# A small sum of the softmax, written as a two-operand addition or as a sum along the free axis, in an attention and feed-forward kernel

## The chip, the core and the metric

The kernel runs on one core of one Trainium2 chip. The metric is the device time of one launch in microseconds; the median of three runs before the change is 1084.55 us (1083.58 to 1084.83). The engines are named as the profile names them: PE is the matrix engine and PEld its weight loads, DVE the vector engine, ACT the scalar engine, POOL the GpSimd engine, SP the queue that issues nearly all DMAs.

## The reference

Causal attention with a decay, over 8 batches, 8 heads, 576 positions and a head size of 64, feeds a gated feed-forward layer (4608 tokens, 512 to 2048 to 512).

```python
scores = scale * np.matmul(q, k.transpose(0, 1, 3, 2))
cum = np.cumsum(np.log(np.clip(f, 0.0001, 1.0)), axis=-1)
decay = cum[:, :, :, None] - cum[:, :, None, :]
scores = np.where(causal, -1000000000.0, scores + decay)
scores = scores - np.max(scores, axis=-1, keepdims=True)
attn = np.exp(scores)
attn = attn / (np.sum(attn, axis=-1, keepdims=True) + 1e-09)
...
h = x @ w_in
sp = np.maximum(h, 0.0) + np.log1p(np.exp(-np.abs(h)))
return ((h * erf(sp)) @ w_out).astype(np.float32)
```

The change is in one place of it: the addition of 1e-09 to the sums of the exponentials, ahead of the division.

## The kernel before, in words

The launch has two stages. The first, up to about 331 us of the trace, is the attention. The second is the feed-forward layer, whose matmuls fill the rest.

The attention walks over 64 steps t. Two heads make a pair p, and each pair has two steps: an even one with the query blocks 4 and 1 (half 0) and an odd one with the blocks 3, 2 and 0 (half 1); j names the head of the pair. The work of one step is spread over several rounds of the loop `for t in range(NH + 2)`, so that in one round the engines work on different steps:

- `scores(t)` on PE (L528, L535) writes the scores of both heads into two PSUM buffers `s`.
- `reduce(t, j)` on DVE (L559) adds the decay, takes the running minimum and writes the scores to the SBUF tile `pr`. Its row extremum goes to part 0 of the small tile `st`. Each L559 is followed by a short read of the accumulator under the same line.
- `exps(t - 1, j)` on ACT (L571) makes the exponentials in place and writes their row sums to part 1 of `st`.
- `normalize(t - 2)` on DVE adds 1e-9 to part 1 (L576) and writes the reciprocals to part 2 (L578); then POOL multiplies `pr` by them (L582).
- `transposes(t - 3, a)` on PE (L594) and `evacuate` on ACT (L599, L603) or DVE (L601) bring the probabilities to the tile `pt`.
- `values(t - 4)` on PE (L621) multiplies by the values into the one PSUM buffer `o`.
- `store(t - 5)` on DVE copies `o` to the SBUF tile `xo` (L630 after an even step's result, L633 and L634 after an odd one's), and SP sends `xo` to DRAM.

Beside this the weights of the feed-forward layer are put together from 64-bit words: DVE runs `words` (L377 to L379) and `joined` (L386, L395), POOL subtracts and adds (L406, L414, L424), ACT rounds (L401, L418). This is called conversion work below. From step 23 on POOL and ACT also prepare the first inputs of the feed-forward layer (L132, L138, L143).

All engines run their instructions in the order in which the loop writes them; no scheduler moves them. On DVE one round is: `normalize`, `store`, `reduce(t, 0)`, `reduce(t, 1)`, in odd rounds an L601, then conversion work if some is due. In this order an instruction that is late on DVE makes all behind it late.

`st` is one tile of 32 columns for each step, with two buffers for each half. Its first 6n columns (n = 2 or 3 blocks) are read as three parts of 2n. The constant is a tile `edge` of 24 columns, set once at the start (L336).

Of the kernel before, what the change touches and what calls it, by code (L numbers as in the profile page):

```python
# [11 lines left out]
F32 = mybir.dt.float32  # L12
# [4 lines left out]
ALU = mybir.AluOpType  # L17
# [5 lines left out]
P = 128  # L23
# [11 lines left out]
BLOCKS = [[4, 1], [3, 2, 0]]  # L35
# [32 lines left out]
SOFTPLUS = "softplus"  # L68
MASK = -2.0 ** 33

EDGE = 24
BIG = 3.0e38

TINY = 2.0 ** -15
# [240 lines left out]
def attention_moe(ctx, tc, q2, k2, vp, f, w_in, w_out, out):  # L315
    nc = tc.nc
# [15 lines left out]
    upper = const.tile([P, P], BF16, name="upper")  # L332
    nc.vector.tensor_copy(out=upper, in_=low)
    edge = ctx.enter_context(tc.tile_pool(name="edge", bufs=1, side="right"))
    tiny = edge.tile([P, EDGE], F32, name="edge")
    nc.vector.memset(tiny, 1e-9)  # L336
    cum_d = dram.tile([B * H, S], F32, name="cum_d")
    xt_d = [dram.tile([DM, NW], F32, name=f"xt_d{v}") for v in range(NV)]

# [121 lines left out]
    with ExitStack() as ph:  # L461
        early = ExitStack()
        wk = ph.enter_context(tc.tile_pool(name="wk", bufs=2))
# [14 lines left out]
        pairs, stats, probs, vals, raw_scores, pts, banks, held = {}, {}, {}, {}, {}, {}, {}, {}  # L478
# [40 lines left out]
        def scores(t):  # L519


            p, half = divmod(t, 2)
            q, k = pairs[p][:2]
            s = [ps_s.tile([P, 1024], F32, name=f"s{t}_{j}", tag="s") for j in range(2)]
            for at, i, k0, k1 in PARTS[half]:
                for j in range(2):
                    h = slice(64 * j, 64 * j + 64)
                    nc.tensor.matmul(out=s[j][:, at:at + k1 - k0], lhsT=q[h, PAD + START[i]:PAD + END[i]],  # L528
                                     rhs=k[h, k0:k1], start=i > 0, stop=k1 < END[i] or i == 4 and p > 0)
            for j in range(2):  # L530
                for i in BLOCKS[half]:
                    if i == 3 or i == 4 and p:
                        continue
                    first = max(0, START[i])
                    nc.tensor.matmul(out=s[j][:, SCOL[i] + first:SCOL[i] + END[i]], lhsT=eye,  # L535
                                     rhs=upper[:, first - START[i]:], start=False, stop=True)
            raw_scores[t] = s
            probs[t] = wk.tile([P, TCOLS[half]], F32, name=f"pr{t}", tag=f"pr{half}")
            n = len(BLOCKS[half])
            line = wk.tile([P, 32], F32, name=f"st{t}", tag=f"st{half}")  # L540
            stats[t] = line[:, :6 * n].rearrange("p (a j m) -> p a j m", a=3, j=2)

        def mask(p, i):

# [4 lines left out]
        def row(t, i, j):  # L549

            return probs[t][:, TOFF[i] + j * END[i]:TOFF[i] + (j + 1) * END[i]]
# [21 lines left out]

        def normalize(t):
            st, n = stats.pop(t), len(BLOCKS[t % 2])
            nc.vector.tensor_tensor(out=st[:, 1], in0=st[:, 1], in1=tiny[:, :2 * n].rearrange("p (j m) -> p j m", j=2),  # L576
                                    op=ALU.add)
            nc.vector.reciprocal(out=st[:, 2], in_=st[:, 1])  # L578
            for m, i in enumerate(BLOCKS[t % 2]):
                for j in range(2):  # L580
                    seg = row(t, i, j)
                    nc.gpsimd.tensor_scalar(out=seg, in0=seg, scalar1=st[:, 2, j, m:m + 1], scalar2=1.0,  # L582
                                            op0=ALU.mult, op1=ALU.mult)
# [79 lines left out]
        total = len(work)  # L663
# [16 lines left out]
        for t in range(NH + 2):  # L680
            there = [0 <= t - n < NH for n in range(6)]
            p, half = divmod(t, 2)
# [11 lines left out]
            if there[2]:  # L694
                normalize(t - 2)
# [6 lines left out]
            if there[0]:  # L702
                scores(t)
# [124 lines left out]
```

## Time and profile before

| what | value |
|---|---|
| median of the runs | 1084.55 us (1083.58 to 1084.83, 3 runs) |
| the profiled execution, its own time | 1084.76 us |
| its span, first to last instruction | 1083.0 us |
| busy share of the span: PE, DVE, ACT, POOL | 99%, 77%, 69%, 68% |
| granted PE clock | 0.999 |

The page gives the busy time of each engine over the span and a chain of waits followed back from the last instruction. Further views group instructions by source line, list who waited for whom, give the instructions of one engine in order of time, or give busy times in chosen stretches. In a row such as "x308 | 131.3, 486 | 36.6 <-PE s L535 17.3" stand the count, the busy time in us, the mean of one in ns, the idle time of the engine just ahead of these instructions in us, and what ended most of it.

### The profile page before, as it was taken

To read this page: it belongs to the slowest core of one execution; us is meant where nothing else is said; L and a number is where in the kernel's file an instruction comes from. 1 tells how busy PE (TensorE), PEld (TensorE's weight loads), DVE (VectorE), ACT (ScalarE), POOL (GpSimd) and SP (SyncE) were. 2 spreads that over 40 slices of the span, in tenths; PEclk is the share of its full clock that TensorE was granted. 3 is DMA by queue.
4 is the path that set the end of the run, shared out by engine and by line. 5 is a ranking of instruction groups with operands and counts; after the bars stand their busy time and mean duration, and the time that the engine had idled before them with its cause. 6 is when DMAs were issued, how large, how long until landed. Compare 5 with 4: busy or idle time off the path is not lost.

```text
span 1083.0 us, 21938 instructions
## 1 busy us (share of the span) xinstructions
PE 1071.5 (99%) x7480; PEld 945.5 (87%) x7480; DVE 834.7 (77%) x1875; ACT 745.7 (69%) x1624; POOL 732.0 (68%) x887
## 2 busy tenths in 40 slices
PE   8999999999999999999999999999999999999998
PEld 6888887888889988998899888989998999899987
DVE  6898898888765997888887986685776768676665
ACT  5899888988987666657666666566476656656563
POOL 3777888988864969798787879636454555536322
PEclk9999999999999999999999999999999999999999
DMA  8799987899766597877969777785867768584742
GB/s 285 247 304 311 343 305 251 279 351 350 254 215 226 190 349 280 303 299 287 357 221 364 273 270 271 277 295 204 311 230 264 289 221 323 213 319 182 246 188 97
DMA packets 86191, 293.69 MB, mean 271 GB/s; under 512 B 8896, under 2 KB 25280, under 8 KB 73792
## 3 DMA queue, kind: packets, MB, share of 16 engines
q1 hardware_dynamic: 85936, 292.00, 75.9%
q8 instruction: 60, 0.98, 0.3%
q14 instruction: 51, 0.42, 0.1%
q10 hardware_dynamic: 144, 0.29, 0.1%
HBM read 240.73 MB, written 51.53 MB: 270 GB/s over the span
## 4 chain that ended last, share of the span: by engine, by line
PE 87%; DVE 4%; ACT 3%; DMA 3%; issue 1%; POOL 1%; SPq 0%; DVEq 0%; POOLq 0%; ACTq 0%
PE y L236 34%; PE pha L178 9%; PE phx L178 9%; PE phy L178 9%; PE s L528 7%; PE o L621 7%; PE t L594 5%; PE phb L178 4%; DMA xt_d<-xo 2%; ACT pr L571 1%; PE s L535 1%; POOL pr L582 1%; DVE pr L559 1%; DMA v<-in_vp_dram 1%; ACT pt L603 1%
## 5 line engine op out<-in xcount | busy, mean ns | idle before, releaser
L225 POOL TENSOR_TENSOR gl<-e,gh 128x384 fp32r<-128x384 f32 x192 | 218.2, 1168 | 262.7 <-PE y L236 162.4
L236 PE MATMUL y<-wo,gh 128*128 128x512 f32 x1152 | 356.5, 391 | 0.4 <-DVE ys L257 0.3
L236 PEld LDWEIGHTS y<-wo,gh 128*128 128x128 f32 x1152 | 215.0, 188 | 45.4 <-DVE ys L257 1.7
L236 PE MATMUL y<-wo,gl 128*128 128x512 f32 x576 | 225.1, 391 | 0.0
L257 DVE TENSOR_TENSOR ys<-y,ys 128x512 f32<-128x512 f32 x252 | 172.1, 687 | 55.2 <-PE y L236 53.6
L582 POOL TENSOR_SCALAR pr<-pr,st 128x576 f32<-128x576 f32 (+4 forms) x320 | 167.6, 544 | 49.2 <-ACT pt L603 11.9
L571 ACT ACTIVATE pr<-pr,st 128x576 f32<-128x576 f32 (+3 forms) x320 | 177.1, 560 | 2.2 <-DVE st L559 2.2
L559 DVE CUSTOM_DVE_ANT_0 pr<-s,c 128x576 f32<-128x576 f32 (+3 forms) x320 | 136.6, 487 | 40.9 <-PE s L535 18.4
L224 ACT CAST gh<-e 128x384 fp32r<-128x384 f32 x192 | 94.1, 513 | 67.3 <-DVE e L217 64.9
L207 ACT ACTIVATE e<-u 128x384 f32<-128x384 f32 x144 | 75.0, 523 | 78.2 <-DVE u L184 74.9
L236 PEld LDWEIGHTS y<-wo,gl 128*128 128x128 f32 x576 | 108.1, 188 | 22.8
L178 PE MATMUL pha<-xs,wi 128*128 128x384 f32 x576 | 117.0, 337 | 0.1
L178 PE MATMUL phx<-xs,wi 128*128 128x384 f32 x576 | 115.4, 334 | 0.0
L178 PE MATMUL phy<-xs,wi 128*128 128x384 f32 x576 | 115.3, 334 | 0.0
L528 PE MATMUL s<-k,q 64*128 64x320 f32 (+4 forms) x768 | 113.8, 407 | 1.5 <-DVE st L559 1.1
L603 ACT COPY pt<-t 128x512 f32<-128x512 f32 x158 | 88.6, 582 | 33.5 <-PE t L594 33.4
L207 ACT ACTIVATE e<-pha 128x384 f32<-128x384 f32 x48 | 23.6, 492 | 125.7 <-PE pha L178 125.7
L621 PEld LDWEIGHTS o<-pt,v 128*64 128x64 f32 x1920 | 93.7, 137 | 14.2 <-DVE st L559 6.9
L178 PEld LDWEIGHTS pha<-xs,wi 128*128 128x128 f32 x576 | 102.3, 188 | 4.2 <-DVE u L188 0.4
L621 PE MATMUL o<-pt,v 128*64 128x128 f32 (+1 forms) x1920 | 102.5, 259 | 3.1 <-DVE xo L630 2.9
L528 PEld LDWEIGHTS s<-k,q 64*128 64x128 f32 x768 | 75.0, 186 | 31.3 <-issue 16.0
L594 PE MATMUL t<-ident,pr 128*128 128x128 f32 x800 | 100.9, 275 | 1.3 <-ACT pt L599 0.9
(75 smaller groups left out, 1780.5 us busy)
## 6 DMA issues: line engine op xcount, KB each, us to landing
wi<-wi_d SPq DMA_DIRECT2D x48, 1792.0 KB, 7.5
wo<-wo_d SPq DMA_DIRECT2D x48, 1024.0 KB, 5.6
v<-in_vp_dram SPq DMA_DIRECT2D x32, 576.0 KB, 5.2
r<-xt_d SPq DMA_DIRECT2D x48, 384.0 KB, 8.9
c<-cum_d SPq DMA_DIRECT2D x62, 288.0 KB, 6.9
q<-in_q_dram SPq DMA_DIRECT2D x32, 320.0 KB, 5.7
k<-in_k_dram SPq DMA_DIRECT2D x32, 288.0 KB, 6.0
part_d<-ys SPq DMA_DIRECT2D x36, 256.0 KB, 6.0
```

What stands on the lines that cost most here:

```text
L178: nc.tensor.matmul(out=ps, lhsT=wi[:, w, n, kd], rhs=xs[:, x, kd], start=not part and kd == 0 and i == 0, stop=kd == 1 and i == 2, skip_gr ...
L207: nc.scalar.activation(out=e_, in_=h[c], func=AF.Softplus)
L225: nc.gpsimd.tensor_tensor(out=gl, in0=e_, in1=gh.bitcast(F32), op=ALU.subtract)
L236: nc.tensor.matmul(out=y, lhsT=x[:, cs], rhs=wo[:, i, w], start=i == 0 and n == 0, stop=i == 1 and n == 2)
L257: nc.vector.tensor_tensor(out=ys, in0=y, in1=ys, op=ALU.add)
L528: nc.tensor.matmul(out=s[j][:, at:at + k1 - k0], lhsT=q[h, PAD + START[i]:PAD + END[i]], rhs=k[h, k0:k1], start=i > 0, stop=k1 < END[i] or ...
L559: nc.vector.tensor_tensor_reduce(out=to[:, ::-1] if j else to, in0=score, in1=decay_, scale=-0.125, scalar=BIG, op0=ALU.add, op1=ALU.min, ...
L571: nc.scalar.activation(out=seg, in_=seg, func=AF.Exp, bias=st[:, 0, j, m:m + 1], scale=-1.0, accum_out=st[:, 1, j, m:m + 1])
L582: nc.gpsimd.tensor_scalar(out=seg, in0=seg, scalar1=st[:, 2, j, m:m + 1], scalar2=1.0, op0=ALU.mult, op1=ALU.mult)
L594: nc.tensor.transpose(out=b[:, n * P:(n + 1) * P], in_=probs[t][:, at:at + P], identity=ident)
L603: nc.scalar.copy(out=pt[:, 512 * a:512 * a + 512], in_=b)
L621: nc.tensor.matmul(out=o[h, to:to + width], lhsT=v[:, ch, h], rhs=pt[:, at[j]:at[j] + width], start=n == 0, stop=n == len(parts) - 1, skip ...
```

## The change

The tile of each step and the constant's tile go. In their place stand four tiles that last for the whole stage, used in turn (t modulo 4). Each has two halves of 6n columns: the first holds what `st` held, the second holds 1e-9 everywhere. `normalize` no longer adds two operands. It reads one operand, a view in which the sum and the constant stand beside each other along the innermost axis, and sums along that axis into part 2; the reciprocal is then taken in place there. For n blocks, 2n sums come from 4n read elements.

```diff
-EDGE = 24
...
     edge = ctx.enter_context(tc.tile_pool(name="edge", bufs=1, side="right"))
-    tiny = edge.tile([P, EDGE], F32, name="edge")
-    nc.vector.memset(tiny, 1e-9)
+    lines = [edge.tile([P, 2, 6 * len(BLOCKS[n % 2])], F32, name=f"line{n}") for n in range(4)]
+    for line in lines:
+        nc.vector.memset(line[:, 1], 1e-9)
...
             n = len(BLOCKS[half])
-            line = wk.tile([P, 32], F32, name=f"st{t}", tag=f"st{half}")
-            stats[t] = line[:, :6 * n].rearrange("p (a j m) -> p a j m", a=3, j=2)
+            stats[t] = lines[t % 4][:, 0, :6 * n].rearrange("p (a j m) -> p a j m", a=3, j=2)
...
             st, n = stats.pop(t), len(BLOCKS[t % 2])
-            nc.vector.tensor_tensor(out=st[:, 1], in0=st[:, 1], in1=tiny[:, :2 * n].rearrange("p (j m) -> p j m", j=2),
-                                    op=ALU.add)
-            nc.vector.reciprocal(out=st[:, 2], in_=st[:, 1])
+            total = st[:, 2].rearrange("p j m -> p (j m)")
+            nc.vector.tensor_reduce(out=total, in_=lines[t % 4][:, :, 2 * n:4 * n].rearrange("p w c -> p c w"),
+                                    axis=mybir.AxisListType.X, op=ALU.add)
+            nc.vector.reciprocal(out=total, in_=total)
```

On DVE, in a round with conversion work (L377 to L379, tile `wtop`) ahead of the normalization, these instructions stand before:

```order
L601 COPY pt_432<-t_2_445 128x512
L377 TENSOR_SCALAR wtop_477<-wraw_286 128x512
L378 TENSOR_SCALAR wtop_477<-wtop_477 128x512
L379 TENSOR_SCALAR wtop_477<-wtop_477 128x512
L576 TENSOR_TENSOR st_364<-st_364,edge 128x6
L578 RECIPROCAL st_364<-st_364 128x6
L630 COPY xo_492<-o_452 128x2x128
```

And now, at the same place on DVE, where `line` is one of the four lasting tiles:

```order
L601 COPY pt_433<-t_2_446 128x512
L377 TENSOR_SCALAR wtop_478<-wraw_290 128x512
L378 TENSOR_SCALAR wtop_478<-wtop_478 128x512
L379 TENSOR_SCALAR wtop_478<-wtop_478 128x512
L576 TENSOR_REDUCE line_83<-line_83 128x6
L578 RECIPROCAL line_83<-line_83 128x6
L630 COPY xo_493<-o_453 128x2x128
```

One instruction has another form; nothing has moved past another, here or on any other engine. At the start DVE has four small memsets (L336) in the place of one.

## The prediction

> **What bounds the kernel now.** I read the page first, for what is busy, then the busy times of the two stages, then who waits for whom on PE, and last the one line that the change touches. On the page:
>
> ```profile
> PE 1071.5 (99%) x7480; PEld 945.5 (87%) x7480; DVE 834.7 (77%) x1875; ACT 745.7 (69%) x1624; POOL 732.0 (68%) x887
> ```
>
> PE is the bound. The line that changes runs 64 times, between 17.8 and 327.8 us, so only the attention matters. The busy times of the attention without its start, and of the feed-forward stage (columns: stretch and its length, then PE, PEld, DVE, ACT, POOL, granted clock, DMA share, GB/s):
>
> ```profile
> 20.00:330.00 310.00, 305.54 (x3555) 256.62 (x3554) 257.75 (x943) 269.50 (x828) 250.94 (x438) 1.00 0.86 289
> 330.00:1083.00 753.00, 748.42 (x3827) 675.18 (x3825) 565.09 (x893) 466.04 (x769) 476.96 (x438) 1.00 0.73 264
> ```
>
> In these 310 us PE is busy for 305.54, so 4.46 us is all that PE stands idle there. DVE is busy for 257.75 of 310, that is 83%. DVE is not the bound; it has 52 us to spare, 0.85 us in each of some 61 rounds. PE's waits in the same stretch:
>
> ```profile
> PE o L621 <- DVE xo L630: 2.6, 4, 0.9
> PE t L594 <- ACT pt L599: 0.9, 2, 0.6
> PE s L528 <- DVE st L559: 0.7, 2, 0.4
> PE o L621 <- DVE xo L634: 0.2, 1, 0.2
> ```
>
> DVE ends 3.5 us of them (2.6 + 0.7 + 0.2), ACT 0.9. Whatever the change does for DVE is worth at most about this, as long as the matmuls themselves stay as they are.
>
> **The operation itself.** The two rows of `normalize` on DVE (ns: shortest, median, longest), and the group of the first in the stretch:
>
> ```profile
> L576 DVE TENSOR_TENSOR st<-st,edge x64: 149/165/1390, 17.8 to 327.8; 128x4 f32<-128x4 f32 x32, 128x6 f32<-128x6 f32 x32
> ```
>
> ```profile
> L578 DVE RECIPROCAL st<-st x64: 178/186/193, 18.0 to 328.0; 128x4 f32<-128x4 f32 x32, 128x6 f32<-128x6 f32 x32
> ```
>
> ```profile
> L576 DVE TENSOR_TENSOR st<-st,edge 128x6 f32<-128x6 f32 (+1 forms) x63 | 21.8, 346 | 3.1 <-ACT pr L571 2.2
> L386 DVE SCALAR_TENSOR_TENSOR wtop<-wraw,wtop 128x512 int32<-128x512 int32 x15 | 15.8, 1051 | 0.0
> ```
>
> An addition of 4 or 6 columns takes 165 ns at the median and up to 1390. The mean of 346 is 181 above the median: 63 x 0.181 = 11.4 us of DVE time goes into something other than the addition. The reciprocal, of the same size and next in line, never takes over 193 ns. What the long ones wait for is seen where DVE and POOL stand side by side. First DVE, then POOL, then PE at about 292 us:
>
> ```profile
> 291.73 1.39 DVE L576 TENSOR_TENSOR st<-st,edge 128x4 f32<-128x4 f32 x1
> ...
> 294.07 0.76 DVE L559 CUSTOM_DVE_ANT_0 pr<-s,c 128x576 f32<-128x576 f32 x1 [0.29 <-issue]
> ```
>
> ```profile
> 292.10 1.00 POOL L143 TENSOR_TENSOR xs<-r,xs 128x384 fp32r<-128x384 f32 x1
> ```
>
> ```profile
> 292.20 1.57 PE L528 MATMUL s<-k,q 64*128 64x320 f32 x12
> ```
>
> The addition ends at 293.12, POOL's operation at 293.10. DVE was held until POOL had finished; I call the part above the median a hold. A second one, DVE, POOL and PE at 172 us:
>
> ```profile
> 171.96 0.67 DVE L576 TENSOR_TENSOR st<-st,edge 128x4 f32<-128x4 f32 x1
> ...
> 174.30 0.76 DVE L559 CUSTOM_DVE_ANT_0 pr<-s,c 128x576 f32<-128x576 f32 x1 [1.02 <-POOL pr L582]
> ```
>
> ```profile
> 171.60 1.01 POOL L132 TENSOR_TENSOR r<-r,r 128x384 f32<-128x384 f32 x1
> ```
>
> ```profile
> 172.44 1.56 PE L528 MATMUL s<-k,q 64*128 64x320 f32 x12
> ```
>
> Ends at 172.63 and 172.61. So the hold is real, and it belongs to an instruction with two operands in SBUF beside a POOL instruction that reads SBUF. The Trainium skill, "SBUF — State Buffer", section "Who interferes with whom", says that such a DVE instruction shares a read interface with POOL and is fully blocked by it, and that a sum along an axis never contends on this chip. By that rule the hold goes completely; the trace shows the first half of it in the ends above, and has no such sum to show the second.
>
> **What the change takes off DVE.** The new operation isn't in the trace. It reads one operand of 8 or 12 elements for each partition and writes 4 or 6. Its nearest rows are the addition's shortest (149 ns) and the reciprocal's longest (193); I take 165, the addition's median, and keep both ends. 64 x (149 to 193 less 165) is -1.0 to +1.8 us of DVE time over the whole attention. With the hold gone, DVE does some 11.4 us less in the stretch, 4% of its 257.75. The rule that speaks against the change stands in the Trainium skill, "VectorE: DVE Perf Modes", section "Rules for kernel authors": a sum along an axis on the hot path is called the slowest operation of this engine, to be restructured away. No row here has the operation; over 8 or 12 elements a lower rate per element has little to act on, and a sum that did cost 193 ns would take 1.8 us of the 11.4 back.
>
> **What of this reaches PE.** DVE's first L559 of a round has to wait for the scores. In the two even rounds above it starts 294.07 - 292.20 = 1.87 and 174.30 - 172.44 = 1.86 us after PE began them. Here is an even round without a hold, DVE, then PE:
>
> ```profile
> 101.72 0.16 DVE L576 TENSOR_TENSOR st<-st,edge 128x4 f32<-128x4 f32 x1
> ...
> 104.06 0.76 DVE L559 CUSTOM_DVE_ANT_0 pr<-s,c 128x576 f32<-128x576 f32 x1 [1.19 <-POOL pr L582]
> ```
>
> ```profile
> 102.20 1.57 PE L528 MATMUL s<-k,q 64*128 64x320 f32 x12
> ```
>
> 1.86 again. The holds of 1.39 and 0.67 us made DVE no later for the scores: its idle time ahead of L559 merely shrank from 1.19 to 0.29 and 1.02. The row names POOL as the releaser, but with the same 1.86 behind PE in all three rounds I read the wait as one for PE's scores. The sum of such cover:
>
> ```profile
> L559 DVE CUSTOM_DVE_ANT_0 pr<-s,c 128x576 f32<-128x576 f32 (+1 forms) x308 | 131.3, 486 | 36.6 <-PE s L535 17.3 <-POOL pr L582 10.1 <-issue 4.2
> ```
>
> DVE idles 36.6 us ahead of L559, three times all the holds. A hold counts only in a round in which this cover is used up, which is where conversion work runs ahead of it. The clearest such round is an odd one that begins at 157.63. As a measure first an odd round without a hold, DVE, then PE: L559 comes 99.40 - 97.33 = 2.07 us after PE began the scores.
>
> ```profile
> 99.40 0.62 DVE L559 CUSTOM_DVE_ANT_0 pr<-s,c 128x448 f32<-128x448 f32 x1 [1.00 <-PE s L535]
> ```
>
> ```profile
> 97.33 1.73 PE L528 MATMUL s<-k,q 64*128 64x448 f32 x12
> ```
>
> The round itself, DVE, then PE:
>
> ```profile
> 158.86 1.23 DVE L576 TENSOR_TENSOR st<-st,edge 128x6 f32<-128x6 f32 x1
> 160.12 0.19 DVE L578 RECIPROCAL st<-st 128x6 f32<-128x6 f32 x1
> 160.23 0.43 DVE L630 COPY xo<-o 128x256 f32<-128x256 f32 x1
> 160.57 0.62 DVE L559 CUSTOM_DVE_ANT_0 pr<-s,c 128x448 f32<-128x448 f32 x1
> ```
>
> ```profile
> 157.63 1.73 PE L528 MATMUL s<-k,q 64*128 64x448 f32 x12
> ...
> 162.50 2.02 PE L528 MATMUL s<-k,q 64*128 64x320 f32 x12
> ```
>
> L559 starts 2.94 us after PE's scores, 0.87 late, with a hold of 1.07 just ahead and no idle time between. PE's next scores, which need the buffers that L559 empties, take 2.02 us where 1.57 is usual: 0.45 us lost on PE. That is the one hold whose way to PE I can follow to its end. And the waits of PE for L630 (2.6 us), the largest ones, mostly have another cause, as at 181 us:
>
> ```profile
> 176.82 1.48 DVE L386 SCALAR_TENSOR_TENSOR wtop<-wraw,wtop 128x512 int32<-128x512 int32 x1
> 178.33 1.37 DVE L395 SCALAR_TENSOR_TENSOR wa<-wraw,wtop 128x512 int32<-128x512 int32 x1
> ...
> 180.88 0.16 DVE L576 TENSOR_TENSOR st<-st,edge 128x6 f32<-128x6 f32 x1
> 181.07 0.19 DVE L578 RECIPROCAL st<-st 128x6 f32<-128x6 f32 x1
> 181.18 0.40 DVE L630 COPY xo<-o 128x256 f32<-128x256 f32 x1
> ```
>
> The addition ahead of this L630 took 0.16 us: nothing was held there. DVE was late from two conversion instructions, which this change does not touch.
>
> **The sum.** Own price of the new operation on PE's path: 0 (in covered rounds), at most 1.8 us if every round passed it on. Hold gone: -0.45 us for certain rounds. The three further memsets lie at the start, ahead of DVE's wait for the input `f`:
>
> ```profile
> L470 DVE TENSOR_SCALAR fr<-fr 64x576 f32<-64x576 f32 x1 | 0.5, 452 | 1.3 <-DMA fr<-in_f_dram 1.3
> L336 DVE MEMSET edge<- 128x24 f32 x1 | 0.1, 78 | 0.0
> ```
>
> 3 x 0.078 = 0.23 us within 1.3 us of idle time: nothing, and 0.23 if that input came at once. The lasting tiles bring no new wait across engines: a line is used again four steps later, as the two buffers of each half were, and its last reader, POOL's L582, stands two rounds earlier. POOL gets its reciprocals sooner; no row has PE waiting for POOL. So 1084.76 - 0.45 = 1084.31 for the profiled execution, whose own time lies 0.21 above the median of the runs; against the median 1084.55 - 0.45 = 1084.1 us.
>
> **The rivals.** A measurement of this kernel tells about 0.2% (2.2 us) from no change.
>
> B, faster: DVE's lead builds up. With 11.4 us less to do, DVE comes to the conversion work earlier, and the waits that it ends on PE vanish with the 0.45: 2.6 + 0.45 = 3.05 us, 1081.5. For it: these waits are short (0.9 at most) and the change is worth 0.18 us in a mean round. Against it: they come behind held conversion instructions in rounds where the addition was not held. The end of this road is all of PE's idle time, 4.46 us (1080.1).
>
> C, no gain since it is still held: an instruction with one operand can be held too. L377 has one operand, and yet:
>
> ```profile
> L377 DVE TENSOR_SCALAR wtop<-wraw x32: 415/564/2705, 11.9 to 628.7; 128x512 int32<-128x512 int32 x32
> ```
>
> If the sum behaves like L377 and not like the reciprocal, the holds stay: 1084.55. Against it: the reciprocal, also with one operand, is never held.
>
> D, slower: the hold moves. Today the addition waits POOL's operation out, and what follows meets POOL afresh. Without it DVE reaches its conversion instructions earlier and may meet POOL's work inside rounds that have no cover:
>
> ```profile
> L386 DVE SCALAR_TENSOR_TENSOR wtop<-wraw,wtop x32: 682/1214/1561, 16.4 to 640.8; 128x512 int32<-128x512 int32 x32
> ```
>
> L386 is at 1051 in the mean in the stretch; at its longest each would cost 0.51 us more. If half of the 15 did and passed it on through L630, that is +3.8, less 0.45: 1087.9. It decides once more than 2.7 us of new holds reach PE, five of them. For it: cover is missing just there. Against it: meetings are as likely to become fewer.
>
> **How the numbers follow.** Forecast (holds gone, nearly all of it under cover) 0.56; B 0.24; C 0.10; D 0.10. Forecast and C lie within 0.2%: 0.66; faster 0.24, slower 0.10. The range takes in B's value, 1081.5, and above the forecast up to four of D's new holds (1084.1 + 2.0 = 1086.1).
>
> **What would show it.** Right: the rows of L576 at 149 to 193 ns with none near 1390, DVE's busy time some 11 us down, its idle time ahead of L559 up by most of that, PE's busy time as before, and PE's waits for L630 still about 2.6. Wrong: L576 still up to 1 us (C); PE's waits for L630 gone and PE's idle time in the stretch down by 3 us (B); the means of L386, L377 or L395 clearly up together with those waits (D).

## The result, and the profile after

The changed kernel is slower: 1093.51 us (1093.23 to 1094.16, 4 runs) against 1084.07 us before (1083.45 to 1084.83, 4 runs); the ratio is 1.0088, with a 95% interval of 1.0070 to 1.0105. That is 9.4 us more where 0.45 less was forecast. The changed operation of `normalize` on DVE (ns: shortest, median, longest), and the groups of DVE in the stretch from 20 to 330 us, after the change:

```profile
L576 DVE TENSOR_REDUCE line<-line x64: 147/158/168, 17.9 to 327.5; 128x4 f32<-128x8 f32 x32, 128x6 f32<-128x12 f32 x32
```

```profile
L558 DVE CUSTOM_DVE_ANT_0 pr<-s,c 128x576 f32<-128x576 f32 (+1 forms) x308 | 131.3, 486 | 45.1 <-PE s L535 23.0 <-POOL pr L582 12.0 <-issue 4.5
...
L386 DVE SCALAR_TENSOR_TENSOR wtop<-wraw,wtop 128x512 int32<-128x512 int32 x15 | 17.2, 1145 | 0.0
...
L377 DVE TENSOR_SCALAR wtop<-wraw 128x512 int32<-128x512 int32 x15 | 12.4, 828 | 0.0
...
L576 DVE TENSOR_REDUCE line<-line 128x6 f32<-128x12 f32 (+1 forms) x63 | 10.0, 159 | 3.2 <-ACT pr L570 2.4
```

No sum is held: the longest takes 168 ns where the addition took up to 1390. So the attention is not where the time went. The busy times of the two stages (same columns as before) and PE's waits in the attention say the same:

```profile
20.00:330.00 310.00, 305.79 (x3556) 257.12 (x3556) 247.67 (x943) 269.46 (x828) 250.37 (x439) 1.00 0.85 289
330.00:1083.00 753.00, 752.73 (x3807) 673.51 (x3807) 575.83 (x889) 466.15 (x769) 478.68 (x437) 1.00 0.72 263
```

```profile
PE o L621 <- DVE xo L630: 2.2, 3, 0.9
PE t L594 <- ACT pt L599: 0.9, 2, 0.6
PE s L528 <- DVE line L558: 0.7, 2, 0.4
PE o L621 <- DVE xo L634: 0.2, 1, 0.2
```

In the attention PE idles 310 - 305.79 = 4.21 us, 0.25 less than before, and DVE is busy 10.1 us less. From 330 us on PE is hardly idle (0.27 of 753 us). The row of before for this stretch, in the prediction, takes in the end of the launch, where no matmul is left; a stretch that lies inside the feed-forward stage in both kernels compares them better, first before, then changed:

```profile
345.00:1070.00 725.00, 724.55 (x3632) 654.04 (x3631) 550.81 (x866) 453.92 (x749) 468.55 (x428) 1.00 0.73 266
```

```profile
345.00:1070.00 725.00, 725.00 (x3594) 648.96 (x3594) 558.17 (x857) 446.90 (x737) 469.19 (x427) 1.00 0.73 266
```

PE is busy throughout in both, and yet 3594 matmuls fill the time that 3632 filled. No wait grew; PE's own work became longer. Which work, the page shows in the group of the down projection's matmuls (`down`; L235 is L236 of the kernel before), first of the kernel before, then of the changed one:

```profile
L236 PE MATMUL y<-wo,gh 128*128 128x512 f32 x1152 | 356.5, 391 | 0.4 <-DVE ys L257 0.3
...
L236 PE MATMUL y<-wo,gl 128*128 128x512 f32 x576 | 225.1, 391 | 0.0
L178 PE MATMUL pha<-xs,wi 128*128 128x384 f32 x576 | 117.0, 337 | 0.1
```

```profile
L235 PE MATMUL y<-wo,gh 128*128 128x512 f32 x1152 | 363.5, 397 | 0.0
...
L235 PE MATMUL y<-wo,gl 128*128 128x512 f32 x576 | 228.3, 396 | 0.0
...
L177 PE MATMUL pha<-xs,wi 128*128 128x384 f32 x576 | 116.8, 337 | 0.0
```

The matmuls on `gh` and on `gl` take turns and overlap in time, so the busy times of the two groups can't be added. Taken together, the 1728 matmuls of the down projection keep PE busy for 402.9 us before and 412.6 us after, 9.7 us more; those of the up projection from 330 us on (`ph` in the rows) take 352.9 and 352.2 us. A unit of the down projection is 36 matmuls in a row. In the chain of waits, an undisturbed unit of the kernel before, then one of the changed kernel (start, length):

```profile
643.40 8.20 PE y L236 x36
```

```profile
645.76 8.43 PE y L235 x36
```

36 matmuls take 0.23 us longer, 6.4 ns each, in a loop in which neither code nor order changed. There are 48 units: 48 x 0.23 = 11 us. What did change for this loop is where its tiles lie. The four lasting lines take 512 bytes of each partition where the constant's tile took 96, at the upper end of the memory, and the rings `u`, `e`, `gh` and `gl` of the feed-forward stage (each a set of six buffers used in turn) are laid out downwards from there. They all moved down by 416 bytes. `wo` is laid out from the other end and stayed.

### The profile page after: what moved, and what is told of

The parts are those of the page before. It is cut to its first block, busy times and chain, and to the rows that moved or that the text cites. A ratio compares the mean times of both kernels' runs of the same rounds, so it can differ in the third digit from the quotient of the medians.

```text
span 1091.4 us, 21941 instructions
## 1 busy us (share of the span) xinstructions
PE 1080.7 (99%) x7480; PEld 947.8 (87%) x7480; DVE 838.0 (77%) x1878; ACT 745.7 (68%) x1624; POOL 732.6 (67%) x887
## 4 chain that ended last, share of the span: by engine, by line
PE 91%; ACT 2%; DVE 2%; DMA 2%; POOL 1%; issue 1%; SPq 0%; POOLq 0%; ACTq 0%; DVEq 0%
PE y L235 37%; PE pha L177 9%; PE phy L177 9%; PE phx L177 9%; PE s L528 7%; PE o L621 7%; PE t L594 6%; PE phb L177 5%; DMA xt_d<-xo 2%; ACT pr L570 1%; PE s L535 1%; DVE pr L558 1%; POOL pr L582 1%; ACT pt L603 1%; PE lead L501 1%
## 5 line engine op out<-in xcount | busy, mean ns | idle before, releaser
L235 PE MATMUL y<-wo,gh 128*128 128x512 f32 x1152 | 363.5, 397 | 0.0
L235 PEld LDWEIGHTS y<-wo,gh 128*128 128x128 f32 x1152 | 216.2, 188 | 48.7 <-DVE ys L256 0.4
L235 PE MATMUL y<-wo,gl 128*128 128x512 f32 x576 | 228.3, 396 | 0.0
L582 POOL TENSOR_SCALAR pr<-pr,line 128x576 f32<-128x576 f32 (+4 forms) x320 | 167.2, 543 | 49.1 <-DVE line L578 14.3
L570 ACT ACTIVATE pr<-pr,line 128x576 f32<-128x576 f32 (+3 forms) x320 | 177.1, 561 | 2.3 <-DVE line L558 2.3
L558 DVE CUSTOM_DVE_ANT_0 pr<-s,c 128x576 f32<-128x576 f32 (+3 forms) x320 | 136.6, 486 | 49.8 <-PE s L535 24.1
L235 PEld LDWEIGHTS y<-wo,gl 128*128 128x128 f32 x576 | 108.7, 189 | 26.5
L216 DVE TENSOR_TENSOR e<-e,u 128x384 f32<-128x384 f32 x144 | 116.9, 813 | 0.0
```

The costliest lines, as they stand in the source:

```text
L216: nc.vector.tensor_mul(e_, e_, h_)
L235: nc.tensor.matmul(out=y, lhsT=x[:, cs], rhs=wo[:, i, w], start=i == 0 and n == 0, stop=i == 1 and n == 2)
L558: nc.vector.tensor_tensor_reduce(out=to[:, ::-1] if j else to, in0=score, in1=decay_, scale=-0.125, scalar=BIG, op0=ALU.add, op1=ALU.min, ...
L570: nc.scalar.activation(out=seg, in_=seg, func=AF.Exp, bias=st[:, 0, j, m:m + 1], scale=-1.0, accum_out=st[:, 1, j, m:m + 1])
```

## The experiments

The places come from the allocation of the built kernels. In the table, "distance" is the start of `gh` or `gl` less the start of `wo`, counted modulo 512 bytes (all buffers of these rings lie at multiples of 512 from each other, and so do the slices that the matmuls use). A unit is the length of 36 matmuls in the chain of waits. The words in the first column say what was meant at the time; the distance says what was built. So in e8, "only gh off", the distance of `gl` is new too.

| kernel | distance gh, gl | unit, us | median, us | ratio to before, 95% interval |
|---|---|---|---|---|
| before, run beside each set | 256, 256 | 8.20 | 1084.07 to 1084.30 | 1 |
| changed | 352, 352 | 8.43 | 1093.51 | 1.0088 (1.0070 to 1.0105) |
| e1, old addition in the new place | 352, 352 | 8.43 | 1093.11 | 1.0081 (1.0066 to 1.0096) |
| e2, new sum in the old place | 256, 256 | 8.20 | 1083.98 | 0.9996 (0.9987 to 1.0006) |
| e3, rings 64 above a multiple of 128 | 320, 320 | 8.40 | 1091.86 | 1.0067 (1.0050 to 1.0084) |
| e4, rings 32 above a multiple of 128 | 288, 288 | 8.40 | 1092.36 | 1.0070 (1.0055 to 1.0085) |
| e5, only u and e off the multiples | 384, 384 | 8.37 | 1089.77 | 1.0049 (1.0032 to 1.0066) |
| e8, only gh off | 352, 384 | 8.34 | 1090.17 | 1.0054 (1.0039 to 1.0069) |
| e7, only gl off | 256, 352 | 8.36 | 1089.41 | 1.0046 (1.0031 to 1.0061) |
| e9, before, only wo off | 224, 224 | 8.40 | 1092.47 | 1.0075 (1.0060 to 1.0090) |
| e10, changed, wo moved along | 256, 256 | 8.22 | 1083.97 | 0.9998 (0.9989 to 1.0007) |
| e11, before, wo 256 higher | 0, 0 | 8.20 | 1084.30 | 0.9999 (0.9990 to 1.0008) |
| e12, before, wo 128 higher | 128, 128 | 8.40 | 1092.07 | 1.0069 (1.0054 to 1.0084) |
| e13, e5 with wo 128 higher | 256, 256 | 8.19 | 1084.02 | 0.9997 (0.9987 to 1.0007) |

**First question: the operation or the place?** e1 puts the two-operand addition back and leaves the changed kernel's tiles:

```diff
-            nc.vector.tensor_reduce(out=total, in_=lines[t % 4][:, :, 2 * n:4 * n].rearrange("p w c -> p c w"),
-                                    axis=mybir.AxisListType.X, op=ALU.add)
+            nc.vector.tensor_tensor(out=total, in0=lines[t % 4][:, 0, 2 * n:4 * n], in1=lines[t % 4][:, 1, 2 * n:4 * n],
+                                    op=ALU.add)
```

> The changed kernel's tiles and places, but the addition of two operands is back (it reads the sums and the constant from the two halves of the lasting line). Placement theory: the four lasting lines take 512 bytes of each partition where the constant's tile took 96, and this moves the rings u, e, gh and gl of the feed-forward stage down by 416 bytes, from a multiple of 128 to 96 above one; from there each down-projection matmul comes 6 to 7 ns later. Then this kernel is as slow as the changed one or a little slower: 1093 to 1095 us, a down-projection unit of 36 matmuls at 8.43 us, and the held additions (up to 1.4 us) back in the attention. Operation theory (the sum along the axis, or the earlier end of the attention that it brings, is at fault): back to 1084 to 1085, a unit at 8.20 us.

e2 keeps the sum and brings the rings to multiples of 128 again, by a tile that nothing uses:

```diff
+    fill = edge.tile([P, 24], F32, name="fill")
+    nc.vector.memset(fill, 0.0)
```

> The changed kernel with a tile of 96 bytes more beside the lasting lines, so that the rings lie at multiples of 128 bytes again (512 below where they lay before). Placement theory: 1083.2 to 1084.2, that is the 0.3 to 0.5 us that the attention gains are kept, a down-projection unit at 8.20 us. Operation theory: 1093 to 1094, as the changed kernel.

Both came out as the placement theory has it. In e1 the holds are back and the loss stays; L576 and a unit of e1:

```profile
L576 DVE TENSOR_TENSOR line<-line x64: 148/166/1420, 17.3 to 327.1; 128x4 f32<-128x4 f32 x32, 128x6 f32<-128x6 f32 x32
```

```profile
645.35 8.43 PE y L235 x36
```

In e2 the sum is there and the loss is gone:

```profile
642.48 8.20 PE y L235 x36
```

The operation itself is thus worth 0.9996 of the time before, with 1 inside its interval. The whole loss belongs to where the tiles lie.

**Second question: which places are bad?** e3 and e4 are e2 with a filling tile of 8 and of 16 columns.

> The changed kernel with a tile of 32 bytes more, so that the rings lie 64 bytes above a multiple of 128. If multiples of 64 are what the rings need: 1083 to 1085, a unit at 8.20 us. If only multiples of 128 do: 1090 to 1096. Operation theory: 1093 to 1094 in any place.

> The changed kernel with a tile of 64 bytes more, so that the rings lie 32 bytes above a multiple of 128. If multiples of 64 are what counts, this place is as bad as the changed kernel's (96 above): 1093 to 1094.5, a unit at 8.43 us. If the distance to the next multiple of 128 counts in some other way, it lies elsewhere between 1083 and 1100. Operation theory: 1093 to 1094.

Both are slow, with units of 8.40 us, so a multiple of 64 isn't enough. At that point I took it that multiples of 128 were what the rings need. e4 also tells against DVE as the link. The gate multiplications (`gate`, e<-e,u) are slower in the changed kernel than before, in this order from 345 us on; first before, then changed, then e4:

```profile
L217 DVE TENSOR_TENSOR e<-e,u 128x384 f32<-128x384 f32 x141 | 96.8, 687 | 0.0
```

```profile
L216 DVE TENSOR_TENSOR e<-e,u 128x384 f32<-128x384 f32 x138 | 112.9, 818 | 0.0
```

```profile
L216 DVE TENSOR_TENSOR e<-e,u 128x384 f32<-128x384 f32 x139 | 95.0, 684 | 0.0
```

In e4 they are as fast as before, and its units are slow all the same. Slow gates do not make the loss; what makes them slow, these runs do not show.

**Third question: which tile?** e5, e8 and e7 put one or two rings off the multiples of 128 at a time, by filling tiles between the rings, with the four lines packed into one tile in e5 and e8 to make room. e9 is the kernel before with 8 unused columns ahead of `wo`, and 24 ahead of `ys` (the tile of the results), which keep that at a multiple of 128:

```diff
     moe.wop = ctx.enter_context(tc.tile_pool(name="wop", bufs=1, reuse_waits="tile"))
+    fill = moe.wop.tile([P, 8], F32, name="fill")
+    nc.vector.memset(fill, 0.0)
     moe.yp = ctx.enter_context(tc.tile_pool(name="yp", bufs=1, reuse_waits="tile"))
+    gap = moe.yp.tile([P, 24], F32, name="gap")
+    nc.vector.memset(gap, 0.0)
```

> The sum along the axis, with gh and gl (the down projection's weights as PE loads them) at multiples of 128 bytes and only u and e (which DVE and ACT use) 96 bytes above one; the four lines are packed into one tile for this. Weight theory (PE is late because it loads weights from gh and gl at such places): 1083.5 to 1084.5, a unit of 36 matmuls at 8.20 us. Vector theory (DVE's gate multiplication on e and u is slower there and holds PE up): 1090 to 1094, a unit at 8.43 us, the gates near 0.82 us in the mean.

> Only gh lies 96 bytes above a multiple of 128; u, e and gl lie at multiples. gh gives the weights of 24 of the 36 matmuls of a unit. Weight theory, each load paying by itself: two thirds of the 9.4 us, 1090.3 (1089 to 1092), with the matmuls on gl's weights at 227 ns. If one bad load in a row sets the pace of all: the whole loss, 1092 to 1094. Vector theory: 1084.

> Only gl lies 96 bytes above a multiple of 128; u, e and gh lie at multiples. gl gives the weights of 12 of the 36 matmuls of a unit. Weight theory, each load paying by itself: one third of the 9.4 us, 1087.2 (1086 to 1088.5). If one bad load sets the pace of all: 1092 to 1094. Vector theory: 1084.

> The kernel before (two-operand addition, rings at multiples of 128), with the down projection's other operand, wo, 32 bytes above a multiple of 128; ys stays at one. Weight theory in its narrow form (only PE's weight loads mind the place): 1084 to 1085, a unit at 8.20 us. If the operand that streams through PE minds it in the same way: 1090 or more, all matmuls of a unit later.

Here my theory fell. PE never reads `u` and `e`, and yet e5 lost 5.5 us; `gl` alone lost nearly as much as `gh` alone (5.1 us against 5.9), though it gives half as many weights, and its 1089.41 us lie between the two values expected; and with all rings in their old places a moved `wo` lost 8.2. e8 met its forecast of 1090.3 with 1090.17, but that is luck, since both its rings have a new distance to `wo`. Units of e5, e8, e7 and e9, in this order:

```profile
645.19 8.37 PE y L238 x36
```

```profile
645.01 8.34 PE y L242 x36
```

```profile
644.69 8.36 PE y L239 x36
```

```profile
645.47 8.40 PE y L236 x36
```

The places told why: to leave `u` and `e` alone off a multiple, e5 had moved `gh` and `gl` by 384 bytes, from one multiple of 128 to another. What all slow kernels share, and no fast one, is a distance between `wo` and one of `gh`, `gl` that is not 256. So the new theory is that the distance counts, not the place.

**Fourth question: distance or place?** Four kernels on which the two theories, or the two forms of the new one, differ. e10 is the changed kernel with `wo` 96 bytes higher (24 columns ahead of `wo`, and 8 ahead of `ys` to keep that at a multiple of 128); e11 and e12 are the kernel before with 64 and 32 columns ahead of `wo`; e13 is e5 with 32.

> The changed kernel, its rings where it puts them (96 above a multiple of 128), but wo 96 bytes higher, so that the distance from wo to gh and gl is again 256 above a multiple of 512, as in the kernel before; ys stays at a multiple of 128. Distance theory (PE reads weights and the streaming operand at the same time and is slowed unless their places differ by the right amount): 1083.2 to 1084.5, a unit of 36 matmuls at 8.20 us. Place theory (each operand has to lie at the right multiple by itself): as slow as the changed kernel or slower, 1092 to 1096.

> The kernel before, with wo (and ys behind it) 256 bytes higher: the distance from wo to gh and gl is a multiple of 512, all tiles at multiples of 128. Distance theory: not known for this distance; if steps of 256 are good 1084 to 1085, and otherwise 1089 to 1094. Place theory with multiples of 128: 1084 to 1085.

> The kernel before, with wo (and ys behind it) 128 bytes higher: the distance from wo to gh and gl is 128 above a multiple of 512, all tiles at multiples of 128. Distance theory: slow, 1089 to 1094. Place theory with multiples of 128: 1084 to 1085.

> The run with u and e alone off the multiples of 128, in which gh and gl had in fact moved by 384 bytes too and so changed their distance to wo, with wo 128 bytes higher to bring the distance back to 256 above a multiple of 512. Distance theory: u and e cost nothing, 1083.2 to 1084.7. If u and e matter by themselves: 1088 to 1090, as without the mending.

All four went with the distance. Units of e10, e11, e12 and e13:

```profile
643.53 8.22 PE y L235 x36
```

```profile
642.41 8.20 PE y L236 x36
```

```profile
646.30 8.40 PE y L236 x36
```

```profile
644.45 8.19 PE y L238 x36
```

e10 has no ring and no `wo` at a multiple of 64, and is as fast as the kernel before. e12 has all of these at multiples of 128, and loses 8 us. e13 has `u` and `e` off, and loses nothing. Distances of 0 and 256 are fast; 128, 224, 288, 320, 352 and 384 are slow. `gh` and `gl` are what PE loads as weights, `wo` is what it streams through them; in this loop PE loads the next weights while it still streams, since PEld is busy for 87% of the span beside PE's 99%. That the distance decides is shown by e9 to e13. That the two reads get into each other's way unless they lie a multiple of 256 bytes apart is a reading that fits all fourteen kernels; no run here shows the reads themselves, or what it is in the memory that does so.

None of the versions is measurably faster than the kernel before. e2, e10 and e13 hold the new sum at a good distance, at 0.9996 to 0.9998, each with 1 inside the interval.

## Why the prediction was wrong

- **The hold, and that it goes: right.** The sum takes 147 to 168 ns (149 to 193 was the bound, 165 the value taken). That a sum along an axis is never held, the rule of the Trainium skill, "SBUF — State Buffer", section "Who interferes with whom", is borne out: 36 of the 64 sums overlap a POOL instruction in the trace and none is held, where 27 of the 64 additions took over 200 ns (up to 1390), and e1 brings the holds back (28 over 200, up to 1420). The rule against the change, in the Trainium skill, "VectorE: DVE Perf Modes", section "Rules for kernel authors", that such a sum is the slowest operation, did not matter at 8 or 12 elements: 158 ns at the median, as for the 37 additions that were not held. Rival C is out.
- **11.4 us off DVE, nearly all under cover: right.** DVE's busy time in the stretch fell by 10.1 us, and its idle time ahead of the scores rose by 45.1 - 36.6 = 8.5.
- **The one hold followed to PE: right.** The same round after the change, DVE, then PE:

```profile
159.25 0.15 DVE L576 TENSOR_REDUCE line<-line 128x6 f32<-128x12 f32 x1
159.44 0.19 DVE L578 RECIPROCAL line<-line 128x6 f32<-128x6 f32 x1
159.55 0.42 DVE L630 COPY xo<-o 128x256 f32<-128x256 f32 x1
160.10 0.62 DVE L558 CUSTOM_DVE_ANT_0 pr<-s,c 128x448 f32<-128x448 f32 x1
```

```profile
158.03 1.73 PE L528 MATMUL s<-k,q 64*128 64x448 f32 x12
...
162.90 1.57 PE L528 MATMUL s<-k,q 64*128 64x320 f32 x12
```

  L558 comes 2.07 us after PE's scores, as in a round without a hold, and PE's next scores take 1.57 us where they took 2.02. (L601 stands at the end of the even rounds, not of the odd ones as the description of a round on DVE has it; in the trace of the kernel before it runs at 156.79, and the conversion work ahead of the odd round's addition comes right behind it.)
- **Rivals B and D: small.** PE's waits for L630 went from 2.6 to 2.2 us, so DVE's lead did not build up. Some of the conversion work did become longer (L386 from 1051 to 1145 ns, L377 from 758 to 828: 15 x 0.094 + 15 x 0.070 = 2.5 us of DVE time), and some shorter (L378 from 556 to 502, 15 x 0.054 = 0.8 us), but PE's idle time in the stretch did not grow. D gave the right sign for a reason that did not happen.
- **The step that failed** is the sentence near the start: "The line that changes runs 64 times, between 17.8 and 327.8 us, so only the attention matters." The change also gives memory a new layout, and the layout holds until the end. The prediction named the condition on which its bound rested, "as long as the matmuls themselves stay as they are", and did not look whether it would hold. The lasting tiles were costed by their waits and their memsets alone; that they are 416 bytes larger than what they replace, ahead of everything laid out behind them, was not looked at. In the table this term alone measures 1.0081 (e1), and the term that was worked out measures 0.9996 (0.9987 to 1.0006, e2), an interval that holds the 0.45 us that were forecast and no change as well. In the slow places e1, with the holds, is even 0.4 us below the changed kernel without them (1093.11 against 1093.51). So no run shows that the 0.45 us reach the time of the launch.
- **11 us in units, 9.7 in the matmuls, 9.4 in the time.** 48 x 0.23 takes every unit of the kernel before at 8.20 us. Timed from the starts in its trace, 7 of the 46 units that stand alone take over 8.25 us, and the one at 362.34 in its chain of waits is such a one:

```profile
362.34 8.36 PE y L236 x36
```

  Here DVE ran conversion work (L377 to L379) until 367.0 and added the unit's first `y` to `ys` only then (L257); the unit falls behind at 367.7, so I put its lateness down to DVE. In the changed kernel 1 unit of 46 is over 0.05 us longer than the shortest. What is left between 9.7 and 9.4 I have not accounted for.

## What to carry to other kernels

A change that only resizes a tile in one stage can slow another stage that it does not touch, since later tiles are laid out from where it ends: before costing such a change, compare the places of all tiles in the built kernels, those of the longest loop on the bounding engine first. Where PE is the bound, check the distance between the tile that it loads as weights and the tile that it streams; here the distances 0 and 256, counted modulo 512 bytes, were the fast ones, and a few unused columns (e2, e10) set it right. And when single-tile experiments contradict each other, look at what each of them moved besides.

## What the runs showed of the hardware that was not expected

- 36 matmuls of 128 x 512 with their weight loads take 8.19 to 8.22 us when weights and streaming operand lie 0 or 256 bytes apart modulo 512, and 8.34 to 8.43 us at the other distances tried, without any idle time on PE in the profile and at a granted clock of 1.0. PE's waits from 345 to 1080 us come to 0.3 us before and to none in the changed kernel; only the pace changes.
- It is enough that a third of the weights lie badly: `gl` alone costs 8.36 - 8.20 = 0.16 us a unit, more than two thirds of the 0.23 of all. In its trace (e7) the matmuls on `gh`, whose distance is still 256, start some 232 ns apart as well, where it was 227 before.
- Sums along an axis over pairs (128 x 4 from 128 x 8, 128 x 6 from 128 x 12) take 158 ns at the median, the same as the additions of these sizes that were not held.
